# Experts of a fused attention and MoE kernel: side work placed anew by step, and three PSUM banks in turn for the first layer

## The chip, the cores and the metric

One NeuronCore of a Trainium2 chip runs the whole program. The metric is the time of the device in microseconds (us), as the median of several executions. Engines are named as in the profile: PE is TensorE's matmul and PEld its weight load, DVE is VectorE, ACT ScalarE, POOL GpSimd, SP the engine whose queue issues the DMAs.

## What is computed

Three stages in float32: a gated linear attention over 4 x 8 heads of 768 tokens, a dense MLP with a rational activation, and a mixture of eight experts in which every token passes through every expert and a Sinkhorn normalisation gives the weights of the sum. The change touches the last stage alone:

```python
def _moe2_ref(x, w_gate, w1, w2):          # x 3072 x 384, E = 8, F = 1024
    logits = x @ w_gate
    P = np.exp(logits - logits.max())
    for _ in range(8):
        P /= P.sum(1, keepdims=True) + 1e-09
        P /= P.sum(0, keepdims=True) + 1e-09
        P *= N / E
    for e in range(E):
        h = np.maximum(x @ w1[e], 0.0)
        out += P[:, e:e + 1] * (h @ w2[e])
```

## The kernel before

The attention and the first MLP take the first 830 us or so. Then `experts` runs 8 experts x 6 tiles of 512 tokens; each tile has four steps q = 0 to 3, one for 256 of the 1024 hidden units, so 192 steps s in a row. Numbers are split into a high part that TensorE multiplies in one pass (hi) and the rest (lo), and a product is three matmuls.

The **first layer** of a step multiplies two blocks of weights with two blocks of tokens by a Winograd-like scheme: 11 products (`mul`) of three matmuls of 256 columns, into two PSUM tiles, `ha` and `hc`, of one bank each. ScalarE copies parts (`s1` to `s3`), VectorE adds them up (`z0`, `s5`, `z1`), and `relu` makes hi on ScalarE and lo on VectorE (L1159, L1160). `ha` and `hc` come from one pool of two banks, so `ha` of a step lies in the bank of the `ha` before it, and is free when both halves of `relu(ha)` have read it. The **second layer** of step s - 1 (`old`) runs between the first layer's products of step s: 24 matmuls of 384 columns, let out by `go(old, n)` with n = 6, 8, 8 and 7 (of which 2 are left). After the fourth step of a tile `result` adds the tile's output, weighted by P, to the accumulators.

The order of the instructions on each engine is the order in which the code is written (`manual_schedule`). **Side work** is woven in by hand: `beside(s)` lists streams with a number of slots for this step, `spread` lays the slots out evenly over six places, and `next(place)` in the step lets out those that have come due. In order, the places lie: after `z0` is issued; after `relu(z0)`; after `mul(ha, 7, 7)` and `s2`; after `s5`; after `relu(ha)`; and after `z1`, at the end. The streams are:

- `gate`: logits of the first six tiles, two slots a tile. For 512 tokens three fp32 matmuls with the gate's weights stationary give 8 x 512, ScalarE copies, four transposes bring it to 128 tokens x 8.
- `sinkhorn`: exponentials and eight iterations; 48 slots over steps 18 to 26. An iteration has a slot for the rows, one for the matmul `cs` with ones, one for the columns.
- `x_combine`: the next tile's tokens, their sums and their split: 13 instructions, five slots in each of steps q = 0, 1, 2.
- `expert_load`, `expert_entry`: DMA of a quarter of an expert's weights, and its four sums and five splits, 14 slots in one step. A split is a ScalarE copy and a subtraction (`split`, `g.tt`), which here goes to GpSimd.
- `weights_check`: a test of the first MLP's 32 pieces of weights, three slots each (load; one operation; three operations), about one slot a step from step 28 to step 148.
- `x_load`: DMA of a tile's tokens, two tiles ahead.

The first three entries and the first gate tile are issued ahead of the experts, the entries by a planner that chooses between GpSimd and VectorE by its own costs.

Of the kernel before, what the change touches and what calls it, by code (L numbers as in the profile page):

```python
# [714 lines left out]
def split(g, w, x):  # L715

    v, act, pool, pe, sync = g.eng
    yield act.copy(w[:, 0], x)
    yield g.tt(w[:, 1], x, w[:, 0].bitcast(F32), SUB)
# [173 lines left out]
def chain(*gens):  # L893
    for x in gens:
        yield from x
# [37 lines left out]
def expert_entry(g, n):  # L933

    v, act, pool, pe, sync = g.eng
    yield lambda: n in g.wr
    r = g.wr.pop(n)
    w = yield expert_tiles(g, n)
    x = yield New(g.pws, [128, 3, 128], tag="ws", name=f"ws{n}")

    a11, a21, a12, a22 = (r[:, 0, i] for i in range(4))
    yield v.tensor_tensor(out=x[:, 0], in0=a21, in1=a22, op=ADD)
    yield v.tensor_tensor(out=a21, in0=a11, in1=a21, op=SUB)
    yield v.tensor_tensor(out=x[:, 1], in0=x[:, 0], in1=a11, op=SUB)
    yield v.tensor_tensor(out=x[:, 2], in0=a12, in1=x[:, 1], op=SUB)
    for y, src in zip(w, (r[:, 0, 0:3], r[:, 0, 3:6], x, r[:, 1, 0:3], r[:, 1, 3:6])):
        yield from split(g, y, src)
    g.free(r)
    g.we[n] = w


def gate(g):

    nc = g.nc
    pe, act = nc.tensor, nc.scalar
    g.logits = g.skp.tile([128, NT // 128, 8], F32, tag="logits", name="logits")
    for t in range(NTB):
        ps = g.ps_m.tile([128, 512], F32, tag="m", name=f"lg{t}")
        for k in range(3):
            pe.matmul(ps[:8], g.wg[:, k], g.xs[0, t][:, k].rearrange("p j n -> p (j n)"), start=k == 0, stop=k == 2)  # L960
        lt = g.skp.tile([8, TB], F32, tag="lt", name=f"lt{t}")
        act.copy(lt, ps[:8])
        yield
        ps = g.ps_m.tile([128, 512], F32, tag="m", name=f"lgt{t}")[:, :32].rearrange("p (i e) -> p i e", i=4)
        for i in range(4):
            pe.matmul(ps[:, i], lt[:, i * 128:(i + 1) * 128], g.cst[:8, 0, :8], is_transpose=True, start=True, stop=True)
        act.copy(g.logits[:, 4 * t:4 * t + 4], ps)
        yield


def sinkhorn(g):
    nc = g.nc
    v, act, pool, pe = nc.vector, nc.scalar, nc.gpsimd, nc.tensor
    cst = g.cst
    NB = NT // 128
    ones = g.ones = g.skp.tile([128, 128], F32, tag="ones", name="ones")
    pool.memset(ones, 1.0)
    lg = g.logits
    sh = [128, NB, 8]
    flat = lg.rearrange("p i e -> p (i e)")  # L980

    def psum(nm):
        return g.ps_m.tile([128, 512], F32, tag="m", name=nm)

    def tiny(shape, nm, dt=F32):
        return g.skp.tile(shape, dt, tag=nm, name=nm)

    m = tiny([128, 1], "skm")
    v.tensor_reduce(out=m, in_=flat, axis=mybir.AxisListType.X, op=ALU.max)
    yield  # L990
    ps = psum("mt")
    pe.matmul(ps[:1, :128], m, cst[:, 0], is_transpose=True, start=True, stop=True)
    yield
    m1 = tiny([1, 1], "skm1")
    v.tensor_reduce(out=m1, in_=ps[:1, :128], axis=mybir.AxisListType.X, op=ALU.max)
    yield
    ps = psum("mb")
    pe.matmul(ps[:, :1], ones[0:1], m1, start=True, stop=True)
    yield
    v.tensor_copy(m, ps[:, :1])  # L1000
    x = tiny(sh, "skx")
    v.tensor_scalar(x, lg, m, None, SUB)
    mask = tiny(sh, "skk")
    v.tensor_scalar(mask, x, -87.0, None, ALU.is_ge)
    v.tensor_scalar(x, x, -87.0, None, ALU.max)
    yield
    n = tiny(sh, "skn")
    big = 1.5 * 2.0 ** 23
    v.tensor_scalar(n, x, 1.4426950408889634, big, MULT, ADD)
    v.tensor_scalar(n, n, -big, None, ADD)  # L1010
    yield
    v.scalar_tensor_tensor(out=x, in0=n, scalar=-0.693359375, in1=x, op0=MULT, op1=ADD)
    v.scalar_tensor_tensor(out=x, in0=n, scalar=2.12194440e-4, in1=x, op0=MULT, op1=ADD)
    y = tiny(sh, "sky")
    v.tensor_scalar(y, x, 1.0 / 5040, 1.0 / 720, MULT, ADD)
    for cf in (1.0 / 120, 1.0 / 24, 1.0 / 6, 0.5, 1.0, 1.0):
        v.tensor_tensor(out=y, in0=y, in1=x, op=MULT)
        v.tensor_scalar(y, y, cf, None, ADD)
        yield
    ni = tiny(sh, "ski", I32)  # L1020
    v.tensor_scalar(n, n, 127.0, None, ADD)
    v.tensor_copy(ni, n)
    v.tensor_scalar(ni, ni, 23, None, ALU.logical_shift_left)
    v.tensor_tensor(out=y, in0=y, in1=ni.bitcast(F32), op=MULT)
    P = g.P = tiny(sh, "skp")
    v.tensor_tensor(out=P, in0=y, in1=mask, op=MULT)
    yield
    pf = P.rearrange("p i e -> p (i e)")
    for it in range(8):
        r = tiny([128, NB], "skr")  # L1030
        v.tensor_reduce(out=r, in_=P, axis=mybir.AxisListType.X, op=ADD)
        v.tensor_scalar(r, r, 1e-9, None, ADD)
        v.reciprocal(r, r)
        v.tensor_tensor(out=P, in0=P, in1=bc(r, 2, sh), op=MULT)
        yield
        ps = psum(f"cs{it}")
        pe.matmul(ps[:, :NB * 8], ones, pf, start=True, stop=True)
        yield
        c = tiny([128, 8], "skc")
        v.tensor_reduce(  # L1040
            out=c, in_=ps[:, :NB * 8].rearrange("p (i e) -> p e i", e=8), axis=mybir.AxisListType.X, op=ADD
        )
        v.tensor_scalar(c, c, 1e-9, None, ADD)
        v.reciprocal(c, c)
        v.tensor_scalar(c, c, float(NT // 8), None, MULT)
        v.tensor_tensor(out=P, in0=P, in1=bc(c, 1, sh), op=MULT)
        yield


def experts(g, gt, extra):  # L1050

# [44 lines left out]
    def beside(s):  # L1098

        i, q = steps[s]  # L1100
        e, t = tiles[i]
        out = []
        if q < 2 and i + 1 < NTB:
            out.append((gt, 1))
        if q == 0 and i + 1 < len(tiles):
            side["x"] = each(x_combine(g, i + 1))
        if q < 3 and i + 1 < len(tiles):
            out.append((side["x"], 5))
        if q == 1 and i + 2 < len(tiles):
            out.append((each(x_load(g, i + 2)), 1))  # L1110

        if t == NTB - 1 and e + 1 < NE:
            n = (e + 1) * NP2 + q
            if q > 1:
                out.append((each(expert_entry(g, n - 2)), 14))
            out.append((each(expert_load(g, n)), 2))
        if t == 0 and q < 2 and e:
            out.append((each(expert_entry(g, e * NP2 + q + 2)), 14))
        if s == 0:
            out.append((each(expert_load(g, 3)), 2))  # L1120
        if s == 1:
            out.append((each(expert_entry(g, 3)), 14))
        for first, last, x, n in extra:
            if first <= s < last:
                out.append((x, n * (s + 1 - first) // (last - first) - n * (s - first) // (last - first)))
        return out
# [11 lines left out]
    for s, (i, q) in enumerate(steps):  # L1138
# [5 lines left out]
            direct(expert_entry(g, n))  # L1144
        w, x = g.we[n], g.xc[i]
        old = layer2(s - 1, hl) if s else iter(())
        ha, hc = (g.ps_h.tile([128, 2, TB // 2], F32, tag="h", name=f"h{c}{s}") for c in "ac")

        def mul(out, wi, xi, start=False):
            a, b = (w[wi // 3][:, l, wi % 3] for l in range(2)), (x[:, l, xi] for l in range(2))  # L1150
# [14 lines left out]
        mul(ha[:, 1], 4, 3)  # L1165
        act.copy(s1, ha[:, 0])
        v.tensor_tensor(out=z[0][:, 0], in0=ha[:, 1], in1=s1, op=ADD)  # L1167
        next(place)
        go(old, 6)
        mul(hc[:, 0], 6, 5, True)  # L1170
        relu(z[0][:, 0], 0, 0)
        next(place)
        mul(ha[:, 0], 7, 7)
        act.copy(s2, ha[:, 0])
        next(place)
        go(old, 8)
        mul(ha[:, 0], 1, 6)
        act.copy(s3, ha[:, 0])  # L1178
        v.tensor_tensor(out=s5, in0=hc[:, 0], in1=s3, op=ADD)  # L1179
        next(place)  # L1180
        go(old, 8)
        mul(ha[:, 0], 3, 8)
        mul(ha[:, 0], 5, 3)
        relu(ha[:, 0], 0, 1)
# [3 lines left out]
        mul(hc[:, 1], 5, 4)  # L1188
        v.tensor_tensor(out=z[1][:, 0], in0=hc[:, 0], in1=s2, op=ADD)
        v.tensor_tensor(out=z[1][:, 1], in0=hc[:, 1], in1=s5, op=ADD)  # L1190
        go(old, 7)
        next(place)
        relu(z[1], 1, slice(0, 2))
        hl = list(zip(hi, lo))
# [4 lines left out]
def weights_check(g):  # L1199
# [5 lines left out]
    for n in range(2 * NF):  # L1205
# [6 lines left out]
        pf = pat.bitcast(F32)  # L1212
        yield
        v.tensor_tensor(out=hi, in0=hi, in1=pf, op=ALU.max)
        v.scalar_tensor_tensor(out=pf, in0=pf, scalar=0.0, in1=pf, op0=ALU.is_equal, op1=ALU.max)
        v.tensor_tensor(out=lo, in0=lo, in1=pf, op=ALU.min)
        yield
    v.tensor_reduce(out=g.chk[:, 2:3], in_=lo, axis=mybir.AxisListType.X, op=ALU.min)
# [227 lines left out]
def second_mlp(g, check):  # L1446
# [6 lines left out]
    g.pacc = opn("pacc")  # L1453
    g.ph = opn("ph")
    g.acc = {i: g.pacc.tile([128, DM], F32, tag=f"acc{i}", name=f"acc{i}") for i in range(NT // 128)}
    g.ps_m = opn("ps_m", 2, space=PSUM)
    gt = gate(g)
    for _ in range(2):
        next(gt)
    if 0 not in g.xc:  # L1460
        direct(x_combine(g, 0))
    n = NTB * NP2
    extra = [(n - 6, n + 3, sinkhorn(g), 48)]
    if check:
        extra.append((n + 4, n + 124, chain(weights_check(g), verdict(g)), 112))
    with g.tc.manual_schedule():
        experts(g, gt, extra)


def kernel_body(tc, g):  # L1470
# [161 lines left out]
```

## Time and profile before

| what | us |
|---|---|
| median of 3 runs | 2500.05 |
| the 3 runs | 2495.10 to 2504.39 |
| profiled execution, its own time | 2502.43 |
| span of that profile | 2500.6 |
| first matmul of the experts' first step, from the span's start | 828.1 |
| first matmul of their last step | 2480.9 |

Times in rows are microseconds from the first instruction of the profiled execution. Where a row of the timeline or of a group has a bracket or an idle time with an arrow, it is what the engine waited for last. A step is bounded by the first matmul of its first layer (`ha`, L695) and that of the next.

### The profile page before, as it was taken

Reading aid. Unit: us, or ns where it says so; the run is one execution under the profiler, and the core shown is the slowest. Engines: PE = TensorE matmul, PEld = TensorE weight load, DVE = VectorE, ACT = ScalarE, POOL = GpSimd, SP = SyncE. Lnnn points to the kernel's source line nnn. Section 1 sums busy time; section 2 is a strip of 40 time slices with the busy share of each in tenths; the row PEclk is TensorE's granted clock in tenths of the full one; section 3 lists DMA queues with packets and bytes.
Section 4 is the critical chain, followed back from the end, with each engine's and each line's share of the span. In section 5 each row is a group of like instructions: output and inputs, shape, how many; then the busy total and the mean of one; then the engine's idle time right before and its main releaser. Section 6 shows DMA issues by size and latency. Waiting matters only on the chain.

```text
span 2500.6 us, 42922 instructions
## 1 busy us (share of the span) xinstructions
PE 2304.2 (92%) x16783; PEld 2204.6 (88%) x16783; DVE 1731.2 (69%) x3917; ACT 1221.9 (49%) x2764; POOL 381.4 (15%) x374
## 2 busy tenths in 40 slices
PE   1476899999999999889999999999999999999998
PEld 0466788888999899789989999999999999999998
DVE  7788989999986644766675675666566656556554
ACT  3465677777767544343343343344334334335332
POOL 2233232323220100120030020012003003003000
PEclk9787999999999999999999999999999999999999
DMA  3443333333322101111211111212012011011110
GB/s 114 135 121 102 96 102 95 90 92 108 93 86 92 58 26 32 32 45 45 64 64 39 52 70 39 64 39 70 26 64 70 32 51 52 26 52 39 51 39 27
DMA packets 137973, 162.28 MB, mean 65 GB/s; under 512 B 31648, under 2 KB 108960, under 8 KB 137760
## 3 DMA queue, kind: packets, MB, share of 16 engines
q1 hardware_dynamic: 137760, 159.45, 20.5%
q8 instruction: 133, 2.18, 0.4%
q14 instruction: 80, 0.66, 0.1%
HBM read 131.11 MB, written 28.31 MB: 64 GB/s over the span
## 4 chain that ended last, share of the span: by engine, by line
PE 71%; DVE 18%; DMA 4%; ACT 3%; issue 2%; SPq 1%; POOL 0%; DVEq 0%; ACTq 0%; POOLq 0%
PE ye L1077 29%; PE ha L695 7%; PE ha L697 6%; PE ha L696 6%; PE x L325 5%; PE h L325 4%; PE hc L696 3%; PE hc L697 3%; PE hc L695 3%; DVE m L325 3%; DVE lo L1160 1%; ACT m L325 1%; DVE f L325 1%; PE t L325 1%; PE sc L325 1%
## 5 line engine op out<-in xcount | busy, mean ns | idle before, releaser
L1077 PE MATMUL ye<-we,hi 128*128 128x384 f32 x3072 | 697.8, 339 | 0.0
L1077 PEld LDWEIGHTS ye<-we,hi 128*128 128x128 f32 x3072 | 519.5, 189 | 3.6 <-issue 3.4
L695 PE MATMUL ha<-xc,we 128*128 128x256 f32 x1344 | 393.7, 293 | 18.4 <-DVE lo L1160 9.4
L1077 PE MATMUL ye<-we,lo 128*128 128x384 f32 x1536 | 394.4, 338 | 0.0
L1159 ACT ACTIVATE hi<-z 128x256 fp32r<-128x256 f32 (+1 forms) x384 | 201.7, 525 | 376.5 <-DVE z L1190 252.8
L697 PE MATMUL ha<-xc,we 128*128 128x256 f32 x1344 | 379.3, 282 | 0.0
L696 PE MATMUL ha<-xc,we 128*128 128x256 f32 x1344 | 378.7, 282 | 0.0
L196 POOL TENSOR_TENSOR we<-rawe,we 128x384 fp32r<-128x384 f32 x116 | 127.0, 1114 | 1327.5 <-ACT we L196 1322.7
L1160 DVE SCALAR_TENSOR_TENSOR lo<-z,hi 128x256 fp32r<-128x256 f32 (+1 forms) x384 | 217.8, 567 | 139.1 <-ACT hi L1159 139.0
L695 PEld LDWEIGHTS ha<-xc,we 128*128 128x128 f32 x1344 | 252.8, 188 | 43.7 <-DVE z L1167 19.8
L1077 PEld LDWEIGHTS ye<-we,lo 128*128 128x128 f32 x1536 | 268.6, 189 | 0.0
L1179 DVE TENSOR_TENSOR s<-hc,s 128x256 f32<-128x256 f32 x192 | 81.4, 424 | 268.8 <-ACT s L1178 268.1
L696 PEld LDWEIGHTS ha<-xc,we 128*128 128x128 f32 x1344 | 254.3, 189 | 0.0
L697 PEld LDWEIGHTS ha<-xc,we 128*128 128x128 f32 x1344 | 253.3, 188 | 0.0
L1160 DVE SCALAR_TENSOR_TENSOR lo<-ha,hi 128x256 fp32r<-128x256 f32 x192 | 81.2, 423 | 203.5 <-ACT hi L1159 203.4
L695 PE MATMUL hc<-xc,we 128*128 128x256 f32 x768 | 217.2, 283 | 1.6 <-DVE s L1179 1.6
L696 PE MATMUL hc<-xc,we 128*128 128x256 f32 x768 | 216.8, 282 | 0.0
L697 PE MATMUL hc<-xc,we 128*128 128x256 f32 x768 | 216.3, 282 | 0.0
L1159 ACT ACTIVATE hi<-ha 128x256 fp32r<-128x256 f32 x192 | 73.7, 384 | 288.8 <-PE ha L697 288.8
L1178 ACT COPY s<-ha 128x256 f32<-128x256 f32 x192 | 71.6, 373 | 233.3 <-PE ha L697 233.3
L325 DVE SCALAR_TENSOR_TENSOR m<-m,co,m 128x512 f32<-128x512 f32 x192 | 146.7, 783 | 16.2 <-ACT m L325 16.0
L695 PEld LDWEIGHTS hc<-xc,we 128*128 128x128 f32 x768 | 144.8, 188 | 2.0 <-DVE s L1179 1.9
(348 smaller groups left out, 4553.1 us busy)
## 6 DMA issues: line engine op xcount, KB each, us to landing
xs<-x2g SPq DMA_DIRECT2D x48, 768.0 KB
rawe<-in_moe_w SPq DMA_DIRECT2D x64, 384.0 KB
kqd<-kq SPq DMA_DIRECT2D x48, 384.0 KB
raw<-kqd SPq DMA_DIRECT2D x48, 384.0 KB
raw<-in_moe_w_in SPq DMA_DIRECT2D x48, 128.0 KB
raw<-in_moe_w_out SPq DMA_DIRECT2D x16, 384.0 KB
rawc<-in_moe_w_in SPq DMA_DIRECT2D x16, 384.0 KB
rawc<-in_moe_w_out SPq DMA_DIRECT2D x16, 384.0 KB
```

The lines of the kernel that those rows point to most:

```text
L196: y.fn(*y.args, **y.kw)
L325: ins = op.fn(*op.args, **op.kw)
L695: pe.matmul(out, w[0], x[0], start=start, stop=False, **kw),
L696: pe.matmul(out, w[0], x[1], start=False, stop=False, **kw),
L697: pe.matmul(out, w[1], x[0], start=False, stop=stop, **kw),
L1077: yield pe.matmul(ys[j], x[:, f, c], w[f][:, l], start=q == 0 and n == 0, stop=q == NP2 - 1 and n == 5)
L1159: act.activation(hi[j][:, f], src, AF.Relu)
L1160: v.scalar_tensor_tensor(out=lo[j][:, f], in0=src, scalar=0.0, in1=hi[j][:, f].bitcast(F32), op0=ALU.max, op1=SUB)
L1178: act.copy(s3, ha[:, 0])
L1179: v.tensor_tensor(out=s5, in0=hc[:, 0], in1=s3, op=ADD)
```

## The change

- Three PSUM banks take turns for `ha` and `hc` (tile number 2s + k, every third in a pool of its own); the pool for the small matmuls shrinks from two banks to one.
- `mul(hc, 6, 5)` moves ahead of the first place, and the second layer is let out by 8, 7, 7 and 3.
- `gate`: now the tokens are stationary and the gate's 8 columns move, 12 fp32 matmuls for 512 tokens, no transposes, one slot a tile.
- `sinkhorn`: columns and the next rows in one slot, an empty slot after them, then the matmul; 66 slots over steps 17 to 27.
- `x_combine`: 2, 4, 4, 3 slots in a middle tile's steps, 4, 9, 0, 0 in an expert's last tile, 0, 3, 1, 9 in its first (not in expert 0).
- `expert_entry`: the five subtractions on VectorE; in an expert's first tile the two entries get 3 slots in step 0, 11 in step 1, and 14 in step 2.
- `weights_check`: five slots a piece, one operation each; four slots in each of steps 1 to 3 of the middle tiles from expert 1 on.

```diff
@@ expert_entry
     for y, src in zip(w, (r[:, 0, 0:3], r[:, 0, 3:6], x, r[:, 1, 0:3], r[:, 1, 3:6])):
-        yield from split(g, y, src)
+        yield act.copy(y[:, 0], src)
+        yield v.tensor_tensor(out=y[:, 1], in0=src, in1=y[:, 0].bitcast(F32), op=SUB)
@@ gate
-        ps = g.ps_m.tile([128, 512], F32, tag="m", name=f"lg{t}")
-        for k in range(3):
-            pe.matmul(ps[:8], g.wg[:, k], g.xs[0, t][:, k].rearrange("p j n -> p (j n)"), start=k == 0, stop=k == 2)
...
-        yield
...
+        ps = g.ps_m.tile([128, 512], F32, tag="m", name=f"lg{t}")[:, :32].rearrange("p (i e) -> p i e", i=4)
         for i in range(4):
-            pe.matmul(ps[:, i], lt[:, i * 128:(i + 1) * 128], g.cst[:8, 0, :8], is_transpose=True, start=True, stop=True)
+            c = slice(i % 2 * 128, i % 2 * 128 + 128)
+            for k in range(3):
+                nc.tensor.matmul(ps[:, i], g.xs[0, t][:, k, i // 2, c], g.wg[:, k], start=k == 0, stop=k == 2)
@@ sinkhorn, in the loop of eight
         v.tensor_tensor(out=P, in0=P, in1=bc(r, 2, sh), op=MULT)
         yield
+        yield
         ps = psum(f"cs{it}")
...
         v.tensor_tensor(out=P, in0=P, in1=bc(c, 1, sh), op=MULT)
-        yield
@@ experts, beside
-        if q < 2 and i + 1 < NTB:
+        if q == 0 and i + 1 < NTB:
             out.append((gt, 1))
...
-        if q < 3 and i + 1 < len(tiles):
-            out.append((side["x"], 5))
+        if i + 1 < len(tiles):
+            out.append((side["x"], ((0, 3, 1, 9) if t == 0 and e else (4, 9, 0, 0) if t == NTB - 1 else (2, 4, 4, 3))[q]))
...
         if t == 0 and q < 2 and e:
-            out.append((each(expert_entry(g, e * NP2 + q + 2)), 14))
+            side[q] = each(expert_entry(g, e * NP2 + q + 2))
+        if t == 0 and e:
+            out += [(side[k], n) for k, n in (((0, 3),), ((0, 11),), ((1, 14),), ())[q]]
+        if check and 0 < t < NTB - 1 and 0 < e and q:
+            out.append((check, 4))
@@ experts, the step
-        ha, hc = (g.ps_h.tile([128, 2, TB // 2], F32, tag="h", name=f"h{c}{s}") for c in "ac")
+        ha, hc = ((g.ps_h2 if (2 * s + k) % 3 == 2 else g.ps_h).tile([128, 2, TB // 2], F32, tag="h", name=f"h{'ac'[k]}{s}")
+                  for k in range(2))
...
         v.tensor_tensor(out=z[0][:, 0], in0=ha[:, 1], in1=s1, op=ADD)
+        mul(hc[:, 0], 6, 5, True)
         next(place)
-        go(old, 6)
-        mul(hc[:, 0], 6, 5, True)
+        go(old, 8)
         relu(z[0][:, 0], 0, 0)
...
-        go(old, 8)
+        go(old, 7)
         mul(ha[:, 0], 1, 6)
...
-        go(old, 8)
+        go(old, 7)
         mul(ha[:, 0], 3, 8)
...
-        go(old, 7)
+        go(old, 3)
         next(place)
@@ second_mlp
-    g.ps_m = opn("ps_m", 2, space=PSUM)
+    g.ps_m, g.ps_h2 = (opn(x, 1, space=PSUM) for x in ("ps_m", "ps_h2"))
...
-    extra = [(n - 6, n + 3, sinkhorn(g), 48)]
-    if check:
-        extra.append((n + 4, n + 124, chain(weights_check(g), verdict(g)), 112))
+    extra = [(n - 7, n + 4, sinkhorn(g), 66)]
```

## Rows read from the trace of the kernel before

**Rows 1.** Page, part 1: busy us (share of the span) and instructions.

```profile
PE 2304.2 (92%) x16783; PEld 2204.6 (88%) x16783; DVE 1731.2 (69%) x3917; ACT 1221.9 (49%) x2764; POOL 381.4 (15%) x374
```

**Rows 2.** Stretches: length, busy us by engine, granted clock, DMA share, GB/s.

```profile
870.57:1017.39 146.82, 145.88 (x956) 134.71 (x956) 67.76 (x161) 59.35 (x140) 0.00 (x0) 1.00 0.10 33
1108.60:1279.63 171.03, 167.05 (x1141) 163.36 (x1140) 112.29 (x255) 66.00 (x155) 9.48 (x9) 1.00 0.14 45
1279.63:2480.92 1201.29, 1188.38 (x8153) 1170.18 (x8154) 735.63 (x1640) 485.90 (x1143) 122.68 (x112) 1.00 0.15 49
1722.53:1730.66 8.13, 8.13 (x59) 8.13 (x59) 6.14 (x15) 2.85 (x7) 0.00 (x0) 1.00 0.10 28
```

**Rows 3.** Stretches as before: five Sinkhorn steps, and the second of them.

```profile
1017.39:1081.82 64.43, 50.36 (x302) 48.29 (x302) 49.26 (x138) 23.95 (x57) 14.53 (x14) 0.92 0.12 37
1027.68:1041.59 13.91, 10.71 (x62) 10.21 (x62) 9.22 (x30) 4.54 (x10) 0.00 (x0) 0.88 0.00 0
```

**Rows 4.** Stretches, sum over the first tiles of experts 2 to 7.

```profile
sum 215.11, PE 204.43 PEld 197.91 DVE 147.65 ACT 98.93 POOL 77.45; mean PE 34.07 PEld 32.99 DVE 24.61 ACT 16.49 POOL 12.91
```

**Rows 5.** Waits from 1100 us on: us in total, times, longest us.

```profile
PEld ha L695 <- DVE lo L1160: 17.1, 24, 2.6
PEld ha L695 <- DVE z L1167: 15.9, 50, 0.9
...
DVE wcp L1211 <- DMA rawc<-in_moe_w_out: 0.4, 1, 0.4
```

**Rows 6.** Timeline across the end of a step: start us, us, what, idle before.

```profile
1603.91 0.68 DVE L196 TENSOR_TENSOR xc<-xs,xc 128x512 fp32r<-128x512 f32 x1
...
1604.51 0.42 DVE L1189 TENSOR_TENSOR z<-hc,s 128x256 f32<-128x256 f32 x1
...
1605.29 0.63 ACT L1159 ACTIVATE hi<-z 128x512 fp32r<-128x512 f32 x1 [1.25 <-DVE z L1190]
...
1605.96 0.69 DVE L1160 SCALAR_TENSOR_TENSOR lo<-z,hi 128x512 fp32r<-128x512 f32 x1 [0.70 <-ACT hi L1159]
...
1606.57 0.42 DVE L1167 TENSOR_TENSOR z<-ha,s 128x256 f32<-128x256 f32 x1
...
1607.04 0.19 PEld L695 LDWEIGHTS ha<-xc,we 128*128 128x128 f32 x1 [0.22 <-DVE z L1167]
```

**Rows 7.** Groups from 760 us on: busy us, mean ns, idle before and releaser.

```profile
L196 POOL TENSOR_TENSOR we<-rawe,we 128x384 fp32r<-128x384 f32 x116 | 127.0, 1114 | 1327.5 <-ACT we L196 1322.7
...
L325 DVE TENSOR_TENSOR we<-rawe,we 128x384 fp32r<-128x384 f32 x10 | 5.4, 567 | 2.1 <-ACT we L325 2.0
```

**Rows 8.** Instructions of tile xd from 1085 us: ns, shortest/median/longest.

```profile
L196 DVE TENSOR_TENSOR xd<-xs,xd x80: 415/419/1251, 1111.8 to 2429.1; 128x256 f32<-128x256 f32 x80
```

**Rows 9.** Groups of the gate, then timeline of transposes and of an attention product.

```profile
L960 PE MATMUL lg<-xs,wg 128*8 128x512 f32 x36 | 16.5, 593 | 1.0 <-ACT x2s L325 1.0
...
L966 PE MATMUL lgt<-cst_sb,lt 8*128 8x8 f32 x12 | 1.2, 207 | 0.0
...
839.09 0.41 PE L966 MATMUL lgt<-cst_sb,lt 8*128 8x8 f32 x4 [0.17 <-ACT lt L962]
...
646.74 0.80 PE L325 MATMUL u<-v,raw 128*96 128x48 f32 x8
```

**Rows 10.** Timeline of VectorE: first and last operation of columns, then of rows.

```profile
1028.54 0.35 DVE L1040 TENSOR_REDUCE skc<-cs 128x8 f32<-128x192 f32 x1
...
1029.58 0.36 DVE L1046 TENSOR_TENSOR skp<-skp,skc 128x192 f32<-128x192 f32 x1
...
1030.79 0.34 DVE L1031 TENSOR_REDUCE skr<-skp 128x24 f32<-128x192 f32 x1
...
1031.72 0.36 DVE L1034 TENSOR_TENSOR skp<-skp,skr 128x192 f32<-128x192 f32 x1
```

**Rows 11.** Waits of TensorE, whole span: us in total, times, longest us.

```profile
PE cs L1037 <- DVE skp L1034: 13.1, 8, 2.8
```

**Rows 12.** Timeline of TensorE after a first tile's first step (expert 3).

```profile
1494.49 0.58 PE L695 MATMUL ha<-xc,we 128*128 128x256 f32 x1 [2.26 <-DVE lo L1160]
```

## Prediction of the time, written before the changed kernel ran

> **What bounds the kernel now.** I read first the busy times of the whole run: TensorE 92% [rows 1]. A share over stages with different limits doesn't yet tell what a step is worth, so next I read the experts' stage step by step. A step is 33 first-layer and 24 second-layer matmuls; the 57 back to back take 8.13 us, with TensorE busy for all of it (the last row of [rows 2], whose 59 count one more at either edge). That is the floor that no placing of other work can pass. Against it stand the stretches. Sixteen steps from 870.57 took 146.82 us, 16.7 over 16 x 8.13; five steps from 1017.39 took 64.43, 23.8 over; the twenty of expert 1 after its first tile 171.03, 8.4 over; the last 143 steps 1201.29, 38.7 over [rows 2, 3]. Of these 38.7 the six first tiles of experts 2 to 7 hold 215.11 - 24 x 8.13 = 20.0 [rows 4], the other 119 steps 18.7. With some 2.4 in the rest of expert 1's first tile, about 90 us is all that there is to win behind 870 us, and only this stage is touched.
>
> What are the 90? Behind 1108 us the waits name two releasers, and both are VectorE: the `lo` of `relu(ha)`, which frees the PSUM bank that the next step's first matmul wants (17.1 us in 24 waits), and `z0`, which `mul(ha, 7, 7)` waits for (15.9 us in 50) [rows 5]. (This is the load's idle time, which overlaps the matmul before it, so both are upper ends.) So the kernel is bound by TensorE with VectorE late at two points of the loop. One step shows the second: a 0.68 us subtraction of the tokens' sums sits at the fifth of the six places, ahead of both `z1` additions; these start at 1604.51, then hi, lo and `z0` follow one after the other up to 1606.99, and the weight load comes at 1607.04 after a wait of 0.22 [rows 6]. Between 870 and 1082 us it is the gate's matmuls and the Sinkhorn loop.
>
> **The change, part by part.**
>
> *Three banks.* `ha` of step s+1 gets the bank that `hc` of step s-1 had, read a whole step earlier. The wait on `lo` loses its cause; what is late next is `z0`, which stands behind the same `lo` on VectorE's queue. So I don't count 17.1 as won.
>
> *More cover for `z0`.* Ahead of `mul(ha, 7, 7)` stood 6 second-layer matmuls, now 8. The 57 matmuls stream 33 x 256 + 24 x 384 = 17664 columns in 8.13, so a second-layer one of 384 takes 0.177 and a first-layer one 0.12; the cover grows by 0.35. The 0.22 waited in rows 6 is about what the operation ahead of `z1` costs there, so undisturbed the chain just met its date; with 0.35 more cover I take some 0.4 of lateness as free. The two that move come out of the last place, where only 2 were ever left (6+8+8 of 24, now 8+7+7); the other places lose one each, 0.18 us, against copies of some 0.37 us under over 1.2 us of cover: nothing.
>
> *Sums of tokens.* 13 instructions as before, now 2, 4, 4, 3 by step, which leaves one 0.42 us VectorE operation at the fifth place of step 0 and none in the others; the sixth place lies in the 0.7 us in which VectorE waits for hi. Two or three per tile move over to the last step and are there before their matmuls. The 0.2 that was lost in rows 6 goes.
>
> *Test of weights.* The same 32 pieces, five slots each instead of three, four slots a step in steps 1 to 3 of the middle tiles: single operations of about 0.56 in place of three in a row. Its 32 loads sit on SP's queue ahead of the tokens' and the weights' loads; each can go out as soon as the piece before has been read, four slots ahead of its reader, so about one step. VectorE waited for such a load once, 0.4 us [rows 5]. I cost them at nothing; if that cover were gone, 32 waits of 0.4 to 2 us would be 13 to 64. In step 3 the last place holds two operations (0.68 and 0.56 against 0.7 idle): 0.1 a tile is lost.
>
> *Weights' parts.* 29 entries of 5 subtractions, all now on VectorE: 0.567 each [rows 7], 2.84 an entry, 82 us in all. They leave GpSimd, where one took 1.11. There is a return: while GpSimd works, a 0.42 us VectorE operation takes up to 1.25 [rows 8]. With 14 slots in a step, two subtractions fall on the fifth place: `z1` 0.8 late, less the 0.4 that is free, some 0.4 a step for three steps of an expert, and 0.2 for the fourth, where 11 slots and three of the tokens' share it. I take 1.6 in a first tile, all in, in place of 3.3 (20.0/6): 10.5 won over six. Bounds: 2.84 for each entry if all of it is on the path (below), and the whole 20.0.
>
> *Gate.* Before, 6 matmul records of 512 columns, 2.75 us a tile (16.5/6), and four transposes, 0.41 [rows 9]. After, 12 fp32 matmuls, two records each, every record with a load of 128 columns of weights and 8 columns moving. None such is in the trace. Nearest in shape are the transposes (128 columns loaded, 8 moving): four take 0.41 with 0.207 for one, so (0.41 - 0.207)/3 = 0.068 from one to the next. The other end is 0.10, eight records with 48 columns in 0.80. 24 x 0.068 = 1.6, up to 2.4. I take 1.7, nearer to the transposes, since few columns move. Won: 1.45 a tile, six tiles, 8.7 (4.6 at the other end).
> The Trainium skill ("TensorE: Matmul & The Clock Gate", section LDWEIGHTS) has a rule that speaks against this: a load takes columns/1.2 ns whatever the rows, so 107 ns for 128 columns. By it the gate would be 24 x 0.107 = 2.6 us, an estimate from that page, and the tile would win 0.6 in place of 1.45. The transposes' 0.068 is already under that figure, so the trace speaks for the smaller one.
>
> *Sinkhorn.* One iteration is 9 small VectorE operations, 1.40 for the columns and 1.29 for the rows [rows 10], and a matmul that now comes two places later instead of one. Column and row now stand in one block of 2.7. TensorE waited 13.1 us for eight of these [rows 11], and after such waits the granted clock averages 0.88 in a step of 13.91 [rows 3], which is half clock for a part of it. After: the block after `z0` is due 1.8 us of TensorE work later, so 0.9 or more is still waited there; the block in the second half has 3.4 us and waits little. Steps 20 to 23 hold two iterations each: 5.4, beside 3.0 of the step's own (67.76 in sixteen steps [rows 2] is 4.2, less 1.2 for the sums), 1.5 to 3.9 of sums and entries; VectorE has 10 to 12.3 us in a step, and with about 1 idle the four steps take 49, 16.2 over the floor; step 24 is free. Before 23.8 in five; won about 7 (bounds 0 and 14: nothing gained where VectorE is full; half the waits and dips gone).
>
> *The rest.* Two to three us may be lost at the handover, where 5 subtractions that GpSimd had now stand on VectorE's queue; I take 1.
>
> **The sum.** Gate 8.7, less 0.9 for the Sinkhorn's head moved into the gate's last steps, 7.8; Sinkhorn 7; expert 1's twenty steps from 8.4 to 4, 4.4; first tiles 10.5; the other 119 steps from 18.7 to 8 (0.2 a middle tile, 0.7 a last one), 10.4; handover -1. Together 39. The profiled execution took 2502.43 us (span 2500.6), the median is 2500.05; against it 2461.
>
> **The rivals.**
> *The late one moves on* (0.12). Banks help nothing by themselves if VectorE is late because its queue is full: the 2.26 us wait at 1494.49 for `lo` [rows 12] came after one step with results, entry, sums and three test operations in a row, and `z0` stands behind that `lo`. Then the waits change their name, and entries on VectorE eat the rest: gate 7.8 and 5 to 10 elsewhere, 2482 to 2487. For it: both waits have one queue. Against it: the step of rows 5 was 0.2 late because of one operation at one place.
> *VectorE becomes the bound* (0.07; slower). One mechanism: the 28 entries of these tiles stand in order on VectorE's queue ahead of `z1`, in the last two steps of an expert and the first three of the next. If all 2.84 of each came onto the path, 79.5 and 4.8 for the middle tiles would stand where 38.7 stand now: 45.6 more, less the 18 won elsewhere (7.8 + 7 + 4.4 - 1), so 2528. It decides from (38.7 - 4.8 + 18)/28 = 1.86 us of each entry on. Against it: VectorE is busy 147.65 of 215.11 us in first tiles [rows 4], which leaves 11 us a tile.
> *All waits go* (0.13). If the free 0.4 swallows the fifth places too, first tiles, middle tiles and expert 1 come within 8 us of the floor, and the Sinkhorn wins 12: some 63 won, 2437.
>
> **How the numbers follow.** My forecast, 2445 to 2478, has 0.68, and 2461 as its time. The range takes in most of the better case and the moved-on waits: 2436 to 2486, about 0.82. A measurement of this kernel can tell 0.5%, 12.5 us, from no change: faster means under 2487.5. Faster 0.84, same 0.08, slower 0.08.
>
> **What would show it.** Right: no wait of a first matmul on `lo`; waits on `z0` under 5 us in all, left in steps after entries; middle tiles at 32.6 to 32.9 us; the gate's 24 records in 1.6 to 1.9; no weights' subtraction on GpSimd, and no 1.25 us operation on VectorE; a matmul `cs` of the first half still waiting about 1, that of the second half little. Wrong: first tiles over 36 us, gate records 0.1 apart, VectorE waiting for the test's loads, or steps 20 to 23 over 52 us.

## Result and the profile after

The changed kernel takes 2457.31 us, the kernel before 2498.41 beside it: a ratio of 0.983, 95% interval 0.981 to 0.986. The profiled execution took 2453.49 us, span 2451.7, which is 48.9 less than before; the medians differ by 41.1. (The profiled execution lies 3.8 under the median here, and 4.0 over it in the kernel before.)

The first part of the profile's page gives each engine's busy us, share and instructions: GpSimd has lost its work in this stage [rows 1].

```profile
PE 2282.5 (93%) x16867; PEld 2214.3 (90%) x16867; DVE 1762.2 (72%) x4064; ACT 1222.4 (50%) x2758; POOL 218.5 (9%) x227
```

Stretches of the changed kernel, with the columns of [rows 2]. The first row is the experts' first step; then the sixteen steps with the gate, the five Sinkhorn steps, expert 1 after its first tile, the last 143 steps, and two single middle tiles.

```profile
827.54:849.67 22.13, 20.68 (x113) 19.85 (x112) 9.84 (x25) 7.92 (x19) 0.21 (x1) 0.70 0.35 114
...
874.52:1019.56 145.04, 145.04 (x1015) 144.40 (x1014) 72.44 (x177) 57.91 (x136) 0.00 (x0) 0.98 0.11 34
1019.56:1076.58 57.02, 47.01 (x301) 44.63 (x300) 43.28 (x133) 21.98 (x52) 0.00 (x0) 0.97 0.14 46
1101.34:1265.24 163.90, 163.90 (x1142) 163.59 (x1141) 120.03 (x279) 66.64 (x155) 0.00 (x0) 1.00 0.18 61
1265.24:2433.58 1168.34, 1167.86 (x8155) 1162.21 (x8154) 758.83 (x1739) 488.11 (x1143) 0.00 (x0) 1.00 0.15 49
2279.55:2311.98 32.43, 32.43 (x230) 32.43 (x229) 18.43 (x42) 12.45 (x29) 0.00 (x0) 1.00 0.15 50
1493.99:1526.74 32.75, 32.75 (x229) 32.75 (x229) 21.95 (x51) 12.46 (x29) 0.00 (x0) 1.00 0.24 76
```

The sum over the first tiles of experts 2 to 7, as in [rows 4]:

```profile
sum 199.07, PE 199.04 PEld 195.17 DVE 150.13 ACT 97.26 POOL 0.00; mean PE 33.17 PEld 32.53 DVE 25.02 ACT 16.21 POOL 0.00
```

From 1265 us on TensorE is busy for 1167.86 of 1168.34 us. By stretch, the forecast against what the two profiles show:

| stretch | before | after | won | forecast |
|---|---|---|---|---|
| first four steps (gate of tiles 0, 1; handover) | 42.46 | 46.97 | -4.5 | 1.9 |
| sixteen steps with four gates | 146.82 | 145.04 | 1.8 | 4.9 |
| five Sinkhorn steps | 64.43 | 57.02 | 7.4 | 7 |
| rest of expert 1's first tile | 26.78 | 24.76 | 2.0 | 0 |
| expert 1, other tiles | 171.03 | 163.90 | 7.1 | 4.4 |
| first tiles of experts 2 to 7 | 215.11 | 199.07 | 16.0 | 10.5 |
| the other 119 steps | 986.18 | 969.27 | 16.9 | 10.4 |

The remaining 2 us lie ahead of the first step and behind the last. So the total was met by luck, with two errors of opposite sign: the gate and the first steps lost 2.7 where 6.8 was to be won, and everything behind 1019 us won 49.4 where 32.3 was forecast. The 16.9 of the last row is at the upper end of what the change won there. Four kernels below have the same instructions in these 119 steps (the gate of before, the gate three at a time, two banks, the Sinkhorn's old slots) and take 971.8 to 975.3 for them in place of 969.3, with TensorE at another pace (last section). By these 11 to 14 were won, nearer to the 10.4 that was forecast.

Waits of the weight loads from 1100 us on, then TensorE's wait for the Sinkhorn's sums (us in total, times, longest). Against [rows 5] no load waits for `lo`, and `z0` holds 5.8 instead of 15.9; `cs` waits 9.6 instead of 13.1 [rows 11]. VectorE waited for no load of the test.

```profile
PEld ha L695 <- DVE z L1171: 5.8, 19, 0.3
...
PE cs L1036 <- DVE skp L1032: 9.6, 6, 2.3
```

Groups of instructions: the gate's 144 records, and 116 of the subtractions, now on VectorE at 0.551 us each, where GpSimd took 1.11 [rows 7].

```profile
L196 DVE TENSOR_TENSOR we<-rawe,we 128x384 fp32r<-128x384 f32 x116 | 63.3, 551 | 0.0
...
L962 PE MATMUL lg<-wg,xs 128*128 128x8 f32 x144 | 20.3, 280 | 1.0 <-ACT x2s L325 1.0
```

The timeline of the gate, 24 records each: the first two tiles' in the first step, the third tile's in a later one.

```profile
835.06 4.18 PE L962 MATMUL lg<-wg,xs 128*128 128x8 f32 x24 [0.99 <-ACT x2s L325]
...
841.35 5.12 PE L962 MATMUL lg<-wg,xs 128*128 128x8 f32 x24
...
879.32 2.74 PE L962 MATMUL lg<-wg,xs 128*128 128x8 f32 x24
```

At full clock (2.4 GHz) the gate takes 2.74 us a tile, no less than the old gate's matmuls (2.75), so only the transposes' 0.4 is won. In the first step it takes 4.18 and 5.12: the granted clock averages 0.70 over 22.13 us, which is some 13 us at half (1.2 GHz). The records' starts in the trace lie 0.112 us apart at full clock (but for the first of a block). In the middle of the first block this goes to 0.214: TensorE had waited 0.99 for `x2s` and then run half of these records when the clock fell.

### The profile page after: what moved, and what is told of

Same layout as the page of the kernel before. It is cut to its first block, busy times and chain, and to the rows that moved or that the text cites. A ratio compares the mean times of both kernels' runs of the same rounds, so it can differ in the third digit from the quotient of the medians.

```text
span 2451.7 us, 42925 instructions
## 1 busy us (share of the span) xinstructions
PE 2282.5 (93%) x16867; PEld 2214.3 (90%) x16867; DVE 1762.2 (72%) x4064; ACT 1222.4 (50%) x2758; POOL 218.5 (9%) x227
## 4 chain that ended last, share of the span: by engine, by line
PE 79%; DVE 11%; DMA 4%; ACT 3%; issue 2%; SPq 1%; POOL 0%; DVEq 0%; ACTq 0%; POOLq 0%
PE ye L1075 32%; PE ha L695 7%; PE ha L697 6%; PE ha L696 6%; PE x L325 5%; PE h L325 4%; PE hc L695 4%; PE hc L696 4%; PE hc L697 4%; DVE m L325 2%; ACT m L325 2%; PE sc L325 1%; DVE f L325 1%; PE t L325 1%; DMA raw<-kqd 1%
## 5 line engine op out<-in xcount | busy, mean ns | idle before, releaser
L1075 PE MATMUL ye<-we,hi 128*128 128x384 f32 x3072 | 725.6, 338 | 0.0
L1075 PEld LDWEIGHTS ye<-we,hi 128*128 128x128 f32 x3072 | 531.1, 188 | 0.1
L697 PEld LDWEIGHTS hc<-xc,we 128*128 128x128 f32 x768 | 146.8, 191 | 0.0
L696 PEld LDWEIGHTS hc<-xc,we 128*128 128x128 f32 x768 | 146.2, 190 | 0.0
```

The source lines that it names most:

```text
L696: pe.matmul(out, w[0], x[1], start=False, stop=False, **kw),
L697: pe.matmul(out, w[1], x[0], start=False, stop=stop, **kw),
L1075: yield pe.matmul(ys[j], x[:, f, c], w[f][:, l], start=q == 0 and n == 0, stop=q == NP2 - 1 and n == 5)
```

## Experiments

All but three undo one part of the changed kernel or do one part alone in the kernel before; the second regroups the new gate, and the last two are new. A line of dots in a diff stands for lines that are not shown. Times are medians; the kernel before stood at 2499 to 2501 beside them, the changed kernel at 2457.31.

**The gate of before**

```diff
-            for k in range(3):
-                nc.tensor.matmul(ps[:, i], g.xs[0, t][:, k, i // 2, c], g.wg[:, k], ...)
+            pe.matmul(ps[:8], g.wg[:, k], g.xs[0, t][:, k]..., ...)   # and the transposes
...
```

The first gate tile is again issued whole ahead of the experts, and the Sinkhorn gets 60 slots over steps 18 to 27.

> The changed kernel with the gate of before (gate's weights stationary, 512 tokens moving, four transposes, two slots a tile; the Sinkhorn therefore starts one step later). In the changed kernel the gate's 24 records take 2.7 us at full clock, 0.112 apart, and the granted clock falls to half in the first step (13.65 us at half) and in two of the five gate steps. Theory A: the new gate is a loss, by its price and by the clock that falls around it. Then the experts' first step goes from 22.1 us back to 16.5, the two gate steps of 12.3 to about 11, and the time falls to about 2449. Rival B: the long first step comes from the handover (the subtractions that are now VectorE's), and the gate is worth what was forecast, 1.4 us a tile. Then the first step stays over 20 us and the time rises to about 2465.

Measured: 2454.23, ratio 0.982 (0.980 to 0.984). First step and sixteen gate steps, as stretches:

```profile
829.58:846.02 16.44, 15.28 (x82) 9.94 (x80) 9.54 (x25) 8.81 (x20) 0.21 (x1) 1.00 0.47 154
...
871.29:1015.72 144.43, 144.43 (x956) 133.99 (x956) 68.34 (x162) 59.98 (x140) 0.00 (x0) 1.00 0.11 34
```

The first step is back at 16.44 (16.46 before), with VectorE carrying the handover's subtractions: the handover costs nothing, and the 5.7 us were the new gate and the clock. The whole gained only 3 of the expected 8, within the spread of the runs; in this profile, 5.4 over the median, the five Sinkhorn steps, begun one step later, took 3.8 more, and the other 119 steps of the table 5.8 more, at the slower pace of the last section. The clock bears theory A out over all profiles: in the eight kernels with the new gate in the first steps the first four steps hold 10.2 to 13.7 us at half clock, in the six with the old gate there none.

**The new gate, three matmuls at a time**

```diff
             for k in range(3):
                 nc.tensor.matmul(ps[:, i], g.xs[0, t][:, k, i // 2, c], g.wg[:, k], ...)
-        nc.scalar.copy(g.logits[:, 4 * t:4 * t + 4], ps)
-        yield
+            if i == 3:
+                nc.scalar.copy(g.logits[:, 4 * t:4 * t + 4], ps)
+            yield
...
```

The first tile's gate, issued ahead of the experts in the changed kernel, here falls into their first step, and the second tile's into the second.

> The changed kernel with the same new gate matmuls, but let out three at a time (four slots a tile, spread over a step; the first tile's in the experts' first step, the second's in their second). Same matmuls, same price, 24 x 0.112 = 2.7 us a tile. Theory A, that the clock falls because 24 records of 8 columns stand in one block: no half clock around the gate any more, first two steps together about 8 us shorter, gate steps all at 10.8 to 10.9, time about 2447 to 2450. Rival B, that the half clock has to do with the waits of the handover or with the gate's matmuls as such: the stretches at half clock stay and the time stays at 2457.

Measured: 2460.69, ratio 0.985 (0.983 to 0.986). The second step and a later gate step:

```profile
845.72:859.90 14.18, 14.18 (x83) 14.18 (x83) 5.87 (x16) 4.68 (x12) 0.00 (x0) 0.74 0.19 57
876.47:887.19 10.72, 10.72 (x82) 10.72 (x82) 5.08 (x12) 4.24 (x10) 0.00 (x0) 1.00 0.01 2
```

By time neither theory holds: 3.4 more than the changed kernel, where A had 7 to 10 less and B the same. The first two steps take 31.39 together against 30.36, the sixteen gate steps 142.50 against 145.04, and the other 119 steps 975.25 against 969.27, at the slower pace of the last section. By the clock each theory has half. In the four later gate steps the fall of the clock is gone: 10.72 in each, at clock 1.00, where the changed kernel had 10.86 twice and 12.3 twice. In the first two steps it stays whatever the grouping. That the new gate is needed for it follows from the run above; why it falls there, and not later, is open.

**Two banks**

```diff
-        ha, hc = ((g.ps_h2 if (2 * s + k) % 3 == 2 else g.ps_h).tile(...) for k in range(2))
+        ha, hc = (g.ps_h.tile(...) for k in range(2))
```

> The changed kernel with ha and hc in two banks as before, all else as changed (the third bank lies idle). Theory A, that placing and cover have removed the lateness itself and the third bank holds little: the first matmuls wait for lo of relu(ha) in the steps after entries only, 2 to 5 us in all, time 2457 to 2462. Rival B, that the bank wait was a cause of its own (17 us in the kernel before): 10 to 17 us longer, 2467 to 2474, with waits on lo of over 10 us in the trace.

Measured: 2459.19, ratio 0.983 (0.982 to 0.985): the same as with three, as far as these runs tell. Of a first matmul's wait on `lo` nothing is left in the trace; `hc` waits a little for the bank's last reader, and the waits of `ha` on `z0` are down to 0.2:

```profile
PEld hc L695 <- DVE z L1194: 2.8, 12, 0.2
```

Theory A holds: at the new places no gain of the third bank is seen. The last 143 steps, whose instructions are those of the changed kernel, are 6.2 slower, 5.2 of them with TensorE busy, and the clock at 1.00:

```profile
1264.87:2439.43 1174.56, 1173.08 (x8154) 1169.11 (x8154) 759.26 (x1739) 488.45 (x1143) 0.00 (x0) 1.00 0.15 49
```

**The subtractions back on GpSimd, at the new places**

```diff
-        yield act.copy(y[:, 0], src)
-        yield v.tensor_tensor(out=y[:, 1], in0=src, in1=y[:, 0].bitcast(F32), op=SUB)
+        yield from split(g, y, src)
```

> The changed kernel with the weights' five subtractions on GpSimd as before, at the new places. Theory A, that GpSimd's work slows VectorE's two-input operations (0.42 to as much as 1.25 us) and so was most of what first tiles had over the floor: first tiles go from 33.2 us to 34 to 35, last tiles by about 0.5, time about 2465 to 2470. Rival B, that the gain in first tiles came from the new spreading of the entry (3, 11 and 14 slots) and VectorE only carries more: first tiles get shorter by the 0.3 us that the steps after entries still lose, time about 2452.

Measured: 2455.92, ratio 0.982 (0.981 to 0.984). The first tiles' sum, and `xd` from 1085 us on:

```profile
sum 196.49, PE 196.49 PEld 195.74 DVE 129.66 ACT 99.93 POOL 74.83; mean PE 32.75 PEld 32.62 DVE 21.61 ACT 16.65 POOL 12.47
```

```profile
L196 DVE TENSOR_TENSOR xd<-xs,xd x80: 412/415/419, 1107.0 to 2387.7; 128x256 f32<-128x256 f32 x80
```

Rival B holds: first tiles are 2.6 shorter than with VectorE, without a wait (32.75 each, the slower of the two paces). The operations of which some took up to 1.25 beside GpSimd [rows 8] take 0.42 at most here, although GpSimd works as much (74.83 against 77.45 in first tiles [rows 4]). That they no longer meet at the new places fits this, but it was not traced pair by pair. The Sinkhorn steps took 59.06 in this profile, 2.0 more, half of it waits and half the clock (0.94). So moving the subtractions is no gain of itself. The entry's new slots alone (3, 11 and 14 in place of 14 and 14) were not undone in any run; their share of the 16.0 won in first tiles is not known.

**The order inside the step as before**

```diff
-        mul(hc[:, 0], 6, 5, True)
         next(place)
-        go(old, 8)
+        go(old, 6)
+        mul(hc[:, 0], 6, 5, True)
...
-        go(old, 7)
+        go(old, 8)
...
```

> The changed kernel with the order inside the step as before: 6 second-layer matmuls, then mul(hc, 6, 5), ahead of mul(ha, 7, 7); 8, 8 and 7 after. All side work at its new places, three banks. Theory A, that the 0.35 us of added cover for z0 is what swallows the lateness: the waits on z0 come back, 0.35 in each step after an entry with two subtractions at the fifth place (some 20 of them, 7 us) and 0.2 in the second step of each middle tile (28 of them, 5.6 us), time about 2468 to 2472. Rival B, that the placing alone removed the lateness: waits on z0 stay under 8 us, time 2457 to 2460.

Measured: 2477.63, ratio 0.991 (0.989 to 0.992): 20 us of the 41 are gone. The waits, and the five Sinkhorn steps:

```profile
PEld ha L695 <- DVE z L1171: 17.3, 51, 0.6
```

```profile
1022.10:1084.40 62.30, 50.94 (x301) 49.02 (x301) 43.40 (x133) 21.84 (x52) 0.00 (x0) 0.89 0.13 43
```

Theory A holds, and more than it said: 17.3 of waits are back, first tiles sum to 205.04 (6.0 more), and the Sinkhorn's steps lose 5.3 of their 7.4. Of these 5.3 only 1.4 are idle time of TensorE (62.30 - 50.94 against 57.02 - 47.01); 3.9 are more busy time for the same matmuls, at a clock of 0.89 in place of 0.97.

**The tokens' sums at their old places**

```diff
-            out.append((side["x"], ((0, 3, 1, 9) if t == 0 and e else ... (2, 4, 4, 3))[q]))
+            out.append((side["x"], 5))        # in steps 0, 1, 2
```

> The changed kernel with the tokens' sums at their old places (five slots in each of a tile's first three steps). Theory A: the 0.68 us operation at the fifth place of the second step is now covered by the 0.35 in mul's new order, so middle tiles stay at 32.5 to 32.8 us; the sums meet the entry in first tiles, which lose up to 0.5 each; time 2457 to 2462. Rival B, that the sums' places were the cause of the waits in middle tiles: the third steps go back to 8.4, 28 x 0.27 = 7.6 us, time about 2466.

Measured: 2464.68, ratio 0.986 (0.984 to 0.988). Waits from 1100 us on:

```profile
PEld ha L695 <- DVE z L1171: 10.6, 30, 0.9
PEld ha L695 <- ACT s L1178: 3.0, 12, 0.3
```

By time this is nearer to B, by mechanism it is A: the third steps of middle tiles stay at 8.11 or 8.19, as in the changed kernel, but for the one of 9.25 with the test's last matmul (8.98 there), so the cover swallows the operation at the fifth place. The loss lies where sums meet an entry: first tiles sum to 203.23, 4.2 more, and the third steps of last tiles take 8.31.

**The test of the weights as before**

```diff
-        if check and 0 < t < NTB - 1 and 0 < e and q:
-            out.append((check, 4))
+        extra.append((n + 4, n + 124, chain(weights_check(g), verdict(g)), 112))   # 3 slots a piece
```

> The changed kernel with the test of the weights as before: three slots a piece, three operations of 0.56 us in one slot, about one slot a step from step 28 to 148. Theory A: three in a row are 1.7 us at the fourth place, where 1.7 are free, so they hurt where a sum stands beside them or in first tiles with an entry: first tiles 1 us longer, middle tiles of experts 1 to 5 0.2 to 0.4 each, time about 2464 to 2470. Rival B, that the test never mattered: every stretch as in the changed kernel within 1 us, time 2457.

Measured: 2467.26, ratio 0.986 (0.984 to 0.988). Theory A holds in kind: `z0` is waited for longer and up to 1.1 us at a time, first tiles sum to 202.12 (3.0 more), and expert 1's other tiles take 1.7 more. The 10 us of the medians are not all the test's: in this profile 70 of 96 middle steps have the slower pace of the last section (22 in the changed kernel's), and the five Sinkhorn steps, where the test doesn't run and nothing was changed, took 2.4 more, by the clock (second row: 0.91 in place of 0.97, TensorE busy for 50.09 in place of 47.01), with less idle time than in the changed kernel.

```profile
PEld ha L695 <- DVE z L1169: 14.4, 32, 1.1
...
1021.66:1081.11 59.45, 50.09 (x301) 47.72 (x300) 43.35 (x133) 21.90 (x52) 0.00 (x0) 0.91 0.13 40
```

**The Sinkhorn's slots as before**

```diff
-    extra = [(n - 7, n + 4, sinkhorn(g), 66)]
+    extra = [(n - 6, n + 3, sinkhorn(g), 48)]   # and its yields as before
```

> The changed kernel with the Sinkhorn's slots as before (rows, matmul, columns one place apart; 48 slots over steps 18 to 26). Theory A, that an empty place ahead of the matmul and the block of two is what shortened the five Sinkhorn steps from 64.4 to 57.0: they go back to about 63, time about 2463. Rival B, that these steps are held by VectorE's amount of work and got shorter since GpSimd no longer slows it: 57 to 59 again, time 2457 to 2459.

Measured: 2459.41, ratio 0.982 (0.980 to 0.985). By time rival B: five steps of 57.89 against 57.02, although `cs` waits in all eight places.

```profile
1021.26:1079.15 57.89, 45.74 (x303) 43.45 (x302) 45.62 (x144) 21.82 (x52) 0.00 (x0) 1.00 0.15 48
```

```profile
PE cs L1033 <- DVE skp L1030: 11.7, 8, 2.3
```

The time alone misleads. TensorE's idle time in these steps is 57.89 - 45.74 = 12.15, against 10.01 in the changed kernel and 14.07 in the kernel before [rows 3], so the new order of slots is worth some 2 us of waits, as `cs` says too (11.7 against 9.6). Here no part of the five steps ran at half clock (1.00 against 0.97), which gave 1.3 back. How much of these steps runs at half clock differs from kernel to kernel (0.91 in the run above, which changed nothing in them), so their times don't rank parts. Their idle time does so roughly: 9.4 to 10.9 in the runs with the new slots over the same steps, the new order and no GpSimd, 11.0 with GpSimd at work again, 11.4 with the old order inside the step, 12.2 here. B's reason, GpSimd, isn't shown by that, and the order is hardly clear of the spread.

**Three banks alone, in the kernel before**

```diff
-        ha, hc = (g.ps_h.tile([128, 2, TB // 2], F32, tag="h", name=f"h{c}{s}") for c in "ac")
+        ha, hc = ((g.ps_h2 if (2 * s + k) % 3 == 2 else g.ps_h).tile(...) for k in range(2))
...
```

> The kernel before with one part of the change alone: three banks in turn for ha and hc. Theory A, the late one moves on: the first matmuls no longer wait for lo, but z0 stands behind that lo on VectorE's queue, so of the 16 us that steps lose at their first matmul most comes back at mul(ha, 7, 7); time about 2493 to 2497, waits on z0 up from 15.9 to 25 us. Rival B, that the two waits add up: 16 us less, 2483 to 2485, waits on z0 as before.

Measured: 2499.84, ratio 1.000 (0.999 to 1.001). Theory A in kind, and no gain at all where it had 2 to 6 us:

```profile
PEld ha L695 <- DVE z L1168: 28.5, 60, 2.5
```

The 17.1 us on `lo` [rows 5] are gone, and the waits on `z0` have grown from 15.9 to 28.5.

**The order inside the step alone, in the kernel before**

```diff
+        mul(hc[:, 0], 6, 5, True)
         next(place)
-        go(old, 6)
-        mul(hc[:, 0], 6, 5, True)
+        go(old, 8)
...
```

> The kernel before with one part of the change alone: mul(hc, 6, 5) and 8 second-layer matmuls ahead of mul(ha, 7, 7), then 7, 7 and 3. Theory A, that the added 0.35 us is the larger half of the gain (putting the old order back into the changed kernel cost 20 us): waits on z0 from 15.9 to under 5, third steps of middle tiles from 8.45 to 8.2, time about 2480 to 2484; the waits on lo stay, since the bank is still shared. Rival B, that the cover only helps at the new places: at the old ones VectorE is late by more than 0.35, time 2494 to 2498.

Measured: 2486.71, ratio 0.995 (0.993 to 0.996).

```profile
PEld ha L695 <- DVE lo L1160: 21.3, 26, 3.4
PEld hc L695 <- DVE s L1179: 5.8, 6, 1.6
PEld ha L695 <- DVE z L1167: 3.1, 11, 0.3
...
1011.02:1077.96 66.94, 52.08 (x302) 49.65 (x302) 49.88 (x139) 23.86 (x57) 14.51 (x14) 0.90 0.11 36
```

Theory A in kind: waits on `z0` fall to 3.1. 12.6 us are won, not 16 to 20: the longest lateness moves to `lo` and `s5`, first tiles stay as they were (215.30 against 215.11), and the five Sinkhorn steps (last row) take 2.5 more than in the kernel before. So the cover by itself wins nothing in either stretch.

**Put together**

```diff
+        if t < 2:   # gate of the first two tiles as before, the others three matmuls at a time
...
-        yield v.tensor_tensor(out=y[:, 1], in0=src, in1=y[:, 0].bitcast(F32), op=SUB)
+        yield (pool if n > 5 else v).tensor_tensor(out=y[:, 1], in0=src, in1=y[:, 0].bitcast(F32), op=SUB)
```

> The changed kernel with three things from the runs before put together: the first two tiles' gate as in the kernel before (no half clock in the first steps there), the other four with the new matmuls let out three at a time (10.7 us a gate step, none at half clock), and the weights' subtractions of the entries from number 6 on back on GpSimd, at the new places (first tiles 196.5 in place of 199.1 us). If these add up: first step 16.5 in place of 22.1, gate steps 10.7, first tiles 196.5, time about 2446 to 2449. If the half clock of the first steps comes back or GpSimd's gain is the TensorE pace of that run, 2453 to 2457.

Measured: 2447.97, ratio 0.979 (0.978 to 0.981), so 9 us under the changed kernel. First step, sixteen gate steps, five Sinkhorn steps:

```profile
830.27:846.71 16.44, 15.28 (x81) 9.95 (x80) 9.56 (x25) 8.82 (x20) 0.21 (x1) 1.00 0.47 156
...
872.03:1014.53 142.50, 142.50 (x1015) 141.87 (x1014) 72.64 (x177) 57.65 (x136) 0.00 (x0) 1.00 0.11 34
1014.53:1073.62 59.09, 49.89 (x301) 47.64 (x300) 43.41 (x133) 21.90 (x52) 0.00 (x0) 0.91 0.14 45
```

The parts add up: 16.44, no half clock at the gate, and first tiles at 196.43. What is left over the floor is mostly the Sinkhorn's, 18 us: 9.2 are idle time, and by the clock (0.91) some 5 are lost.

**The Sinkhorn at four slots a step**

```diff
-    extra = [(n - 7, n + 4, sinkhorn(g), 66)]
+    extra = [(n - 7, n + 4, sinkhorn(g), 44)]
```

All else is as in the run above.

> The best kernel so far (e11) with the Sinkhorn's slots at four a step instead of six, so its 40 slots end in step 26 instead of 23 (44 slots over steps 17 to 27). Theory A, that steps 20 to 24 (59 us for five, 18 over the floor, VectorE busy 43) are held by VectorE's amount of work in a step: with a third less of it in each, steps 17 to 27 together lose 6 to 10 us less, time about 2439 to 2443. Rival B, that each matmul cs waits for its block of 2.7 us whatever stands around it: the same eight waits in more steps, steps 17 to 27 within 2 us of before, time 2447 to 2449.

Measured: 2448.52, ratio 0.979 (0.978 to 0.981). Steps 17 to 27 took 109.04 against 109.30. TensorE's waits there:

```profile
PE ha L695 <- DVE z L1184: 3.3, 3, 2.3
PE hc L695 <- DVE s L1196: 3.2, 2, 2.5
PE cs L1049 <- DVE skp L1045: 2.6, 2, 2.1
```

By time B, by mechanism neither: `cs` waits 2.6 in place of 9.0, and `z0` and `s5` have 6.5 in its stead, where the run above had 0.2. Once more the late one moved on. What would shorten these steps stays open; a smaller amount of VectorE work was not tried.

## Why the prediction was right, and where it was not

**The bound and the floor** held: 57 matmuls in 8.13 forecast, 8.11 or 8.19 measured in most steps from 1101 us on.

**Three banks.** The step "the wait loses its cause, I don't count 17.1 as won" was right, and shown: nothing alone, nothing when undone. It is the rival "the late one moves on", true of this part.

**Cover for `z0`.** The mechanism was right, and its share larger than the text let see: 12.6 us alone, 20 when undone (some of the 20 is the clock in the Sinkhorn's steps and the pace). I had given it no term of its own and counted it in the stretches.

**Sums and test.** Both were cost at nothing and only the sums' 0.2 a step was credited. Undone, the medians rise by 7.4 for the sums and by 10 for the test. What the rows put down to them is less, 4.2 and 3.0 in first tiles: the missed term is the meeting of a sum or of a three-operation slot with an entry. The loads, also cost at nothing, were never waited for.

**Weights' parts.** The term was mis-sized: 1.6 us a first tile forecast, 199.07/6 - 4 x 8.11 = 0.7 measured, 0.2 to 0.3 in the first and in the last step of a first tile. The reason behind its gain was wrong too: VectorE's work is not what paid, since on GpSimd the same places are 2.6 us better.

**Gate.** This step failed. I took the transposes' 0.068 from one record to the next, and 0.10 as the upper end; measured is 0.112 at full clock, so my own sign of being wrong, "gate records 0.1 apart", came true. My reading of the second row was at fault: its eight records start 0.085 apart (but for the first), not 0.10, for 96 columns of weights loaded, and 128/96 of that is 0.113. I had compared the columns that move; the two rows agree by those that are loaded. The rule of the Trainium skill ("TensorE: Matmul & The Clock Gate", section LDWEIGHTS), 107 ns for 128 columns whatever the rows, comes within 5 ns of the 0.112 measured at full clock; at half clock the trace has 0.214. I had weighed it against a row of another kind: the transposes over 8 rows start 0.06 to 0.08 apart, under that rule, and why is open. On top came the half clock in the first steps, which the prediction had no term for. Price and clock together made the first step 5.7 us longer, and the first four 4.5.

**Sinkhorn.** 7 forecast, 7.4 measured. The four steps 20 to 23 take 48.4, where 49 was forecast, and step 24 is free (8.6), as forecast. (49 is 16.5 over the floor, not the 16.2 of the text.) Of the 7.4, 4.1 are idle time and 3.4 are busy time at the clock (0.92 before, 0.97 after). The runs above put some 2 us of the idle time down to the slots; the order inside the step, which the term did not name, may hold 1.4 more. The clock's part isn't tied to either and comes and goes between runs, so that 7.4 came out so near to 7 is in part luck.

**The rivals.** The 0.2 that the text holds against "the late one moves on" is from [rows 6], not 5. "All waits go" came true from 1101 us on: 7.1 + 16.0 + 16.9 = 40 us are won of the 8.4 + 38.7 = 47 that stood over the floor [rows 2], so 7 are left where that rival had 8. That rival's own terms (39.1 for the waits, 12, 7.8 and -1) add up to 58 and not to the 63 it was given, so its time should have been 2442. What kept the execution from it is the gate with the first steps, 9.5 short of the forecast, and the Sinkhorn, 7.4 of that rival's 12. "VectorE becomes the bound" didn't happen: it was busy for 150.13 of 199.07 us in first tiles.

## What to carry to other kernels

When one in-order engine is late and two waits name it, freeing a buffer only renames the wait; what helps is to put more independent work of the bound engine between the late result and its user, here 0.35 us a step for 12.6 us alone and up to 20 of the 41. Place side work by the hole it falls into (an engine waits 0.7 us for hi) and keep single operations apart, before deciding which engine does them. Price a stream of small matmuls by the columns of weights it loads (here 0.112 us for 128, 0.085 for 96), and look at the granted clock around it. Before a stretch's time ranks two kernels, take its idle time and its clock apart.

## What the runs showed that was not expected

The same 57 matmuls have two settled paces with nothing waiting: middle tiles of 32.43 and of 32.75 us in one execution (last two rows of the stretches above), TensorE busy throughout and the clock at 1.00. In the changed kernel's profile 23 of the 96 steps in middle tiles after expert 1 were over 8.16 us, in that with two banks 85. This is worth some 5 us, as much as several of the differences above, so runs within 5 us of each other don't rank parts by themselves; waits and the steps that have them do. What sets the pace is open.

With 24 records of 8 moving columns the granted clock fell to half in the first step, and in two of the four later gate steps (12.3 against 10.86 us); let out three at a time it fell in none of the four later steps (10.72), though still in the first two. With the gate of before it fell in neither. What decides it is open.
